# Attention ahead of the MLP products, in an order worked out by a list scheduler in the source

## The chip, the core and the metric

One core of one Trainium2 chip runs the whole program. The metric is device microseconds from the first to the last instruction of the kernel. TensorE (PE) does the matmuls, VectorE (DVE) and ScalarE (ACT) the element-wise work and the reads of PSUM, GpSimd (POOL) some element-wise work between SBUF tiles, SyncE (SP) issues the DMAs. Each engine runs its own instructions strictly in the order in which they stand in its queue, and waits on semaphores of the others.

## The reference

```
q, k, v: (2, 8, 768, 64) f32     scores = q k^T / 8, keys kept: the first n_sink = 4, and the window of 128
a = softmax(scores);  x = (a v), heads side by side: 1536 tokens x 512
h = x @ w_in (512 x 2048);  g = where(h > 0, h, exp(min(h, 0)) - 1);  x = g @ w_out (2048 x 512)
h = x @ w_in2;              g = max(h, 0) + alpha * min(h, 0);        out = g @ w_out2
```

The four weight matrices arrive as 64-bit floats.

## The kernel before, in words

**Attention.** A work item of attention is a *unit*: one or two blocks of 110 queries (`QB`) of one batch and one pair of heads. There are 32 units with 56 blocks, in the order batch, third of the sequence (`SPLIT`), pair of heads. For each unit PE computes the scores of both heads (tiles `qk`, line 521), DVE adds the mask and takes the row minimum of the negated scores (L529), ACT takes exponentials and their row sum (L534), DVE forms reciprocals (`st`, L544 and L547), POOL scales the rows (L551), PE transposes them against an identity (tiles `t`, L565), DVE or ACT copies the transposes to SBUF (tiles `pt`, L649), PE multiplies them by the values (tiles `x`, L586), and ACT and DVE split the result into a high and a low part (`xh` L594, `xl` L596), 512 rows by 1536 tokens.

**MLP.** Both layers run on split operands: each product is three matmuls (high with high, low with high, high with low; `matmul3`, L293). A *round* takes four of the 16 slices of 128 hidden features (`FG`): for a tile of tokens, four groups `h` of 12 matmuls (`g1`), the activation (`u`, L325 to L335; `gh` on ACT, `gl` on POOL), and four groups `o` of 12 (`g2`), which ACT (round 0) or DVE (L361) adds into `acc`. There are four rounds for each layer, eight in all. Rounds 1 to 7 use three tiles of 512 tokens (`TOK`); round 0 uses five narrower tiles (`TOK0`: 220, 220, 328, 440 and 328 tokens).

**Weights.** Each round needs eight *halves* of weights. A half is loaded as raw 64-bit numbers (L196) and decoded (`decode_w`): two operations on ACT (L267, L268), four on DVE (L270, L273, L276, L279), one on ACT (`wh`, L283), one on DVE (`wl`, L285).

**What sets the order.** While attention runs the order is written by hand (`manual_schedule`): a loop over steps `s` issues the scores of unit `s`, the values of unit `s - 2`, the transposes of unit `s - 1`, and at most one or two groups of round 0's first four tiles from the list `fill`; where there is none yet, `keep_busy` issues matmuls on the identity (L251). A decode that falls on a step issues its DVE operations together. Three softmax buffers (`SB`), five `pt` buffers (`PB`), and four PSUM banks each for `qk` and for everything else are in rotation. Then `mlp_rounds` issues round 0's last tile and rounds 1 to 7; with round 0's last tile it decodes all eight halves of round 1.

Of the kernel before, what the change touches and what calls it, by code (L numbers as in the profile page):

```python
# [11 lines left out]
F32 = mybir.dt.float32  # L12
# [33 lines left out]
NMAX0 = max(n for _, n, _ in TOK0)  # L46
# [17 lines left out]
FILL_MAX = 13  # L64
# [29 lines left out]
VCH = [sum(NCH[lo:hi]) for lo, hi in SPLIT]  # L94

# [18 lines left out]
def attention_mlp2(  # L114
# [38 lines left out]
    def load_kq(g, pool=None, queues=None):  # L153

        b, z, hp = sgs[g]
        nk, nq = KTOT[z], QTOT[z]
        if pool:
            t = pool.tile([P, 2 * max(KTOT)], F32, tag="kq", name=f"kq{g}", bufs=LB)  # L160
        else:
            t = room[:, g * 2 * nk : (g + 1) * 2 * nk]
        for e in range(2):
            rows = slice(e * D, e * D + D)
            lead = 2 * nk if e == 0 else 2 * nq
            c0 = KQ0[z] + e * nk
            src = kq[b, hp, rows, c0 : c0 + nk]
            src = bass.AP(src.tensor, src.offset, [list(src.ap[0]), [lead, 2], [1, nk]])
            (queues or (nc.sync, nc.sync))[e].dma_start(
                out=t[rows, : 2 * nk].rearrange("p (t c) -> p t c", t=2), in_=src  # L170
            )
        keys[g] = t

    def load_v(g, pool=None):
        b, z, hp = sgs[g]
        n = VCH[z] * 2 * D
        if pool:
            t = pool.tile([P, max(VCH) * 2 * D], F32, tag="vr", name=f"vr{g}", bufs=LB)
        else:
            t = room[:, HP * 2 * KTOT[0] + g * n :]  # L180
        nc.sync.dma_start(out=t[:, :n], in_=vc[b, hp, :, V0[z] : V0[z] + n])
# [18 lines left out]

    def load_w_early(g):
        o = HP * (2 * KTOT[0] + VCH[0] * 2 * D) + g * 2 * DM
        load_w(0, g, 0, room[:, o : o + 2 * DM].bitcast(I32).rearrange("p (n t) -> p n t", t=2))

    load_kq(0, queues=(nc.sync, nc.scalar))
    load_kq(1, queues=(nc.sync, nc.scalar))
    load_w_early(0)
    load_kq(2)
    load_w_early(1)
    load_v(0)  # L210
    load_kq(3)
    load_v(1)
# [40 lines left out]
    with tc.tile_pool(name="ps_warm", bufs=1, space=PSUM) as ps_warm:  # L253
        keep_busy(ps_warm, "busy", NWARM)
# [3 lines left out]
    def decode_w(wdec, pool, m, fc, io):  # L258
# [29 lines left out]
    def matmul3(out, pairs):  # L288
        n = 3 * len(pairs)
        i = 0  # L290
        for ah, al, bh, bl in pairs:
            for a, c in ((ah, bh), (ah, bl), (al, bh)):
                nc.tensor.matmul(out, a, c, start=(i == 0), stop=(i == n - 1))  # L293
                i += 1

    class Mlp:
# [3 lines left out]
        def __init__(self, gp, ps):  # L300
            self.gp, self.ps = gp, ps
            self.g, self.narrow = {}, 0

        def g1(self, m, c0, n, fc):
            t, big = c0, max(n, NMAX0)
            xh, xl = (x[:, :, c0 : c0 + n] for x in xs)
            wh, wl = wtiles[m, fc, 0]
            hp = self.ps.tile([P, 512], F32, tag="ps", name=f"h{m}_{t}_{fc}")[:, :n]
            matmul3(
# [7 lines left out]
            def after():  # L317
                u = tmp.tile([P, big], F32, tag="u", name=f"u{m}_{t}_{fc}")[:, :n]
                a, w, bufs = ("n", self.narrow, 2 * FG) if n <= self.narrow else ("", big, None)
                gh, gl = (  # L320
                    self.gp.tile([P, w], F32R, tag=f"g{c}{a}", name=f"g{c}{m}_{t}_{fc}", bufs=bufs)[:, :n]
                    for c in "hl"
                )
# [21 lines left out]
        def g2(self, m, c0, n, r, d):  # L345
            t = c0
            a = acc[:, d, c0 : c0 + n]
            po = self.ps.tile([P, 512], F32, tag="ps", name=f"o{m}_{t}_{r}_{d}")[:, :n]
# [6 lines left out]
            matmul3(po, pairs)  # L355
# [21 lines left out]
    def run(pieces):  # L377

        pend = []
        for p, extra in pieces:  # L380
            if p is None:
                done(pend.pop(0)())
                continue
            if extra:
                extra()
            pend.append(p())
# [10 lines left out]
    def mlp_rounds(mlp, items, wpools, wdec):  # L397
# [18 lines left out]
        for h in order[:2]:  # L416
            load_w(*h[1:])
        state = {"at": 0}

        def weights_step():  # L420
            j = state["at"]
            if j + 2 < len(order):
# [5 lines left out]
        for n, it in enumerate(items):  # L428
            mine = [lambda i=i, it=it: g1(*it, i) for i in range(FG)] + late
            late = [lambda d=d, it=it: g2(*it, d) for d in range(KC)]  # L430
            if n == 0:
                mine += [None] + late
                late = []
            step = len([p for p in mine if p]) // max(1, len(todo[it]))
            for j, p in enumerate(mine):
                if p is not None and todo[it] and j % step == 0:
# [5 lines left out]
        run(pieces)  # L442
# [7 lines left out]
    def distance(blk, pool=None):  # L450

        if pool:
            rel = pool.tile([P, 4 * QB], F32, tag="pt", name=f"rel{blk}", bufs=PB).bitcast(I32)
# [38 lines left out]
    def fast_path():  # L492
        outer = ExitStack()
        ps_qk = outer.enter_context(tc.tile_pool(name="ps_qk", bufs=4, space=PSUM))
        ps = outer.enter_context(tc.tile_pool(name="ps", bufs=4, space=PSUM))
        inner = ExitStack()
        ga = inner.enter_context(tc.tile_pool(name="ga", bufs=FG))
        at = inner.enter_context(tc.tile_pool(name="at", bufs=2))
        at2 = inner.enter_context(tc.tile_pool(name="wdec", bufs=2))
        mlp = Mlp(ga, ps)  # L500
        mlp.narrow = TOK0[0][1]
        soft, trans = {}, {}
        wraw.update(wfirst)
# [327 lines left out]
```

## Time and profile before

| what | value |
|---|---|
| median of 3 runs | 660.78 us (660.52 to 662.04) |
| span of the profiled execution | 660.5 us |
| PE, DVE, ACT, POOL busy | 96%, 66%, 48%, 31% of the span |
| bytes read from HBM | 49.01 MB |

The page gives no other time of the profiled execution than its span; the runs lie 0.0 to 1.5 us above it, their median 0.3 us. Busy time counts a pipelined matmul to its modelled end, so consecutive matmuls overlap in it; what a matmul really costs in a row of them is the distance from one start to the next.

### The profile page before, as it was taken

How to read it: one execution, taken by the hardware profiler on the slowest of the kernel's cores; microseconds unless marked ns; L12 is line 12 of the kernel's file. 1: busy time of each engine (PE TensorE's matmuls, PEld its weight loads, DVE VectorE, ACT ScalarE, POOL GpSimd, SP SyncE). 2: the span in 40 equal slices, each digit the busy share in tenths (PEclk: the TensorE clock that was granted, in tenths of full speed). 3: DMA queues.
4: the chain of work that ended last, by engine and by line, in shares of the span. 5: the costliest groups of instructions: out<-in, count | busy, mean ns of one | idle time of the engine just before them, and what ended most of it. 6: DMA issues, size and time to landing. Idle time of an engine off the chain costs nothing.

```text
span 660.5 us, 9670 instructions
## 1 busy us (share of the span) xinstructions
PE 633.7 (96%) x3444; PEld 526.6 (80%) x3444; DVE 435.9 (66%) x927; ACT 315.7 (48%) x719; POOL 204.4 (31%) x253
## 2 busy tenths in 40 slices
PE   8986899999989899999999999999999999999996
PEld 7775688887977677888888888888888888888885
DVE  5877767655399997768465876694669673343332
ACT  4877466655588675647545733453524230110010
POOL 3354334434123321233215453332123312331130
PEclk9988799999999999999999999999999999999999
DMA  8574336500043343121112211212222000000112
GB/s 256 149 213 140 106 85 167 158 25 1 34 159 127 124 132 128 37 91 64 65 58 70 65 64 44 84 65 65 64 65 64 33 0 1 2 0 1 64 50 83
DMA packets 21659, 52.87 MB, mean 80 GB/s; under 512 B 2658, under 2 KB 9826, under 8 KB 21602
## 3 DMA queue, kind: packets, MB, share of 16 engines
q1 hardware_dynamic: 21024, 51.93, 25.8%
q8 instruction: 29, 0.48, 0.3%
q10 hardware_dynamic: 578, 0.24, 0.2%
q14 instruction: 28, 0.23, 0.1%
HBM read 49.01 MB, written 3.15 MB: 79 GB/s over the span
## 4 chain that ended last, share of the span: by engine, by line
PE 78%; DVE 13%; ACT 4%; issue 2%; POOL 1%; DMA 1%; DVEq 0%; ACTq 0%; SPq 0%; POOLq 0%
PE o L293 36%; PE h L293 34%; PE x L586 3%; DVE wx L276 3%; DVE wx L279 2%; ACT s L534 2%; PE t L565 2%; PE qk L521 2%; DVE wl L285 2%; DVE wx L273 1%; DVE wx L270 1%; DVE pt L649 1%; DVE u L327 1%; DVE acc L361 1%; PE busy L251 1%
## 5 line engine op out<-in xcount | busy, mean ns | idle before, releaser
L340 POOL TENSOR_TENSOR gl<-u,gh 128x512 fp32r<-128x512 f32 (+3 forms) x104 | 133.1, 1280 | 327.6 <-ACT gh L339 322.5
L293 PE MATMUL o<-gh,wh 128*128 128x512 f32 (+3 forms) x416 | 157.3, 380 | 5.5 <-DVE u L327 5.5
L293 PE MATMUL h<-xh,wh 128*128 128x512 f32 (+3 forms) x416 | 158.1, 380 | 1.2 <-ACT xh L594 1.2
L293 PE MATMUL o<-gl,wh 128*128 128x512 f32 (+3 forms) x416 | 156.3, 376 | 1.8 <-POOL gl L340 1.7
L293 PE MATMUL h<-xl,wh 128*128 128x512 f32 (+3 forms) x416 | 156.6, 376 | 0.1
L293 PE MATMUL h<-xh,wl 128*128 128x512 f32 (+3 forms) x416 | 156.4, 376 | 0.0
L293 PE MATMUL o<-gh,wl 128*128 128x512 f32 (+3 forms) x416 | 155.8, 375 | 0.0
L339 ACT CAST gh<-u 128x512 fp32r<-128x512 f32 (+3 forms) x104 | 60.9, 585 | 139.3 <-DVE u L335 114.2
L293 PEld LDWEIGHTS o<-gh,wh 128*128 128x128 f32 x416 | 78.4, 189 | 23.4 <-DVE u L327 8.4
L361 DVE TENSOR_TENSOR acc<-o,acc 128x512 f32<-128x512 f32 x72 | 49.2, 688 | 72.0 <-PE o L293 71.7
L293 PEld LDWEIGHTS h<-xh,wh 128*128 128x128 f32 x416 | 79.2, 190 | 16.9 <-ACT xh L594 1.3
L293 PEld LDWEIGHTS o<-gl,wh 128*128 128x128 f32 x416 | 78.8, 189 | 16.0 <-POOL gl L340 2.9
L293 PEld LDWEIGHTS h<-xl,wh 128*128 128x128 f32 x416 | 79.3, 191 | 13.6 <-DVE xl L596 0.4
L293 PEld LDWEIGHTS h<-xh,wl 128*128 128x128 f32 x416 | 79.4, 191 | 13.4
L293 PEld LDWEIGHTS o<-gh,wl 128*128 128x128 f32 x416 | 78.8, 189 | 13.5
L551 POOL TENSOR_SCALAR s<-s,st 110x250 f32<-110x250 f32 (+5 forms) x112 | 52.6, 487 | 92.3 <-DVE st L547 31.1
L283 ACT CAST wh<-wx 128x512 fp32r<-128x512 f32 x64 | 39.6, 619 | 65.6 <-DVE wx L279 31.7
L534 ACT ACTIVATE s<-s,st 110x250 f32<-110x250 f32 (+5 forms) x112 | 53.1, 477 | 27.1 <-DVE st L529 27.0
L331 DVE TENSOR_SCALAR u<-h,alpha_sb 128x512 f32<-128x512 f32 x48 | 35.9, 748 | 45.6 <-PE h L293 45.6
L279 DVE CUSTOM_DVE_ANT_0 wx<-wx,wq 128x1024 uint16<-128x1024 uint16 x64 | 59.2, 925 | 1.4
L276 DVE SCALAR_TENSOR_TENSOR wx<-wr,wx 128x512 int32<-128x512 int32 x62 | 56.6, 914 | 1.0
L285 DVE TENSOR_TENSOR wl<-wx,wh 128x512 fp32r<-128x512 f32 x64 | 46.8, 733 | 15.5 <-ACT wh L283 13.9
(56 smaller groups left out, 634.5 us busy)
## 6 DMA issues: line engine op xcount, KB each, us to landing
wr<-in_w_dram SPq DMA_DIRECT2D x62, 512.0 KB, 3.6
kq<-in_kq_dram SPq DMA_DIRECT2D x16, 237.0 KB, 4.4
vr<-in_vc_dram SPq DMA_DIRECT2D x8, 384.0 KB, 4.1
out_dram<-acc SPq DMA_DIRECT2D x12, 256.0 KB, 2.0
kq<-in_kq_dram SPq DMA_DIRECT2D x16, 180.0 KB, 3.8
vr<-in_vc_dram SPq DMA_DIRECT2D x8, 256.0 KB, 3.8
acc<-in_w_dram SPq DMA_DIRECT2D x2, 512.0 KB, 5.4
kq<-in_kq_dram SPq DMA_DIRECT2D x8, 110.0 KB, 3.4
```

The source lines that it names most:

```text
L276: nc.vector.scalar_tensor_tensor(out=x, in0=high, scalar=-0x40000000, in1=x, op0=ALU.bitwise_and, op1=ALU.bitwise_or)
L279: nc.vector.tensor_tensor(out=x, in0=x, in1=r, op=ALU.add)
L283: nc.scalar.copy(wh, xf)
L285: nc.vector.tensor_tensor(out=wl, in0=xf, in1=wh, op=ALU.subtract)
L293: nc.tensor.matmul(out, a, c, start=(i == 0), stop=(i == n - 1))
L331: nc.vector.tensor_scalar(out=u, in0=hp, scalar1=0.0, scalar2=alpha_sb[:, fc : fc + 1], op0=ALU.min, op1=ALU.mult,)
L339: nc.scalar.copy(gh, u)
L340: nc.gpsimd.tensor_tensor(out=gl, in0=u, in1=gh, op=ALU.subtract)
L361: nc.vector.tensor_tensor(out=a, in0=po, in1=a, op=ALU.add)
L534: nc.scalar.activation(sb[:n, j, e, :w], sb[:n, j, e, :w], AF.Exp, bias=st[:n, 0, j, e : e + 1], scale=-1.0, accum_out=st[:n, 1, j, e : e ...
L551: nc.gpsimd.tensor_scalar(out=sb[:n, j, e, :w], in0=sb[:n, j, e, :w], scalar1=st[:n, 3, j, e : e + 1], scalar2=1.0, op0=ALU.mult, op1=ALU. ...
L586: nc.tensor.matmul(px[e * D : e * D + D, o : o + n], vr[:r, vs : vs + D], pt[:r, p0 : p0 + n], start=(k == 0), stop=(k == c - 1),)
```

## The change

The hand-written loop over steps is gone, and so are `TOK0` and `fill`. In its place each operation of attention, each weight half's decode (its eight operations one by one) and each load is given to `Plan` with a cost per engine, what it depends on and the buffers that it takes. `Plan.run` repeatedly picks the operation that can start earliest, by rank among those within 40 ns, issues it and books its end. Where PE would be idle for more than 0.7 us plus 128 ns it issues `keep_busy` matmuls. A copy `pt` may go to DVE or ACT. There are five softmax buffers and six `pt` buffers, eight PSUM banks shared by everything, and keys, values and early weights are placed anywhere in the space of `acc` (`Field`), which the MLP uses only later. Only two groups `h` of the first 512-token tile are part of the plan (`EARLY`), each in four parts. After it, `mlp_rounds` runs all eight rounds on 512-token tiles, and spreads the decodes for round 1 over round 0's three tiles. The program's scheduler may still move instructions of those rounds ahead on their engines, as the order below shows.

```diff
-TOK0 = [(0, 220, 0), (220, 220, 1), (440, 328, 2), (768, 440, 4), (1208, 328, 5)]
 TOK = [(c, 512) for c in range(0, NT, 512)]
-UB, SB, PB, LB = 2, 3, 5, 3
-MS = {2: 0, 3: 1, 4: 2}
-DS = [1, 3, 5, 7, 9, 10, 11, 12]
-NWARM, BUSYN = 10, 4
-FILL_MAX = 13
+UB, SB, PB = 2, 5, 6
+NBANK = 8
+BANKS = {"qk": 4, "tx": 4, "h": 2}
+NWARM = 10
+EARLY = 2
+WHEN = [16.0 + 3 * j for j in range(2 * FG)]
...
+class Plan:
+    SIGNAL, DRAIN, LAND, RATE, SLACK, GAP, IDLE = 60.0, 170.0, 1800.0, 230.0, 40.0, 700.0, 128.0
...
+    def best(self, todo):
+        cands = {}
+        for op in todo:
+            if any(d.end is None for d in op.deps) or op.behind and op.behind.end is None:
+                continue
+            asked = [cls.ask(size, len(holds)) for cls, size, *holds in op.takes]
+            if None in asked:
+                continue
+            for eng, cost in op.costs.items():
+                t = max([self.free.get(eng, self.start)] + [got[0] for got in asked])
+                for d in op.deps:
+                    t = max(t, d.end + (0.0 if d.eng == eng else self.SIGNAL))
+                if op.lock and eng in self.locks:
+                    t = max(t, self.locks["POOL" if eng == "DVE" else "DVE"])
+                cands.setdefault(eng, []).append((t, op, cost))
+        picks = []
+        for eng, got in cands.items():
+            first = min(t for t, _, _ in got)
+            t, op, cost = min((c for c in got if c[0] <= first + self.SLACK), key=lambda c: (c[1].rank, c[0]))
+            picks.append((t, op.rank, eng, op, cost))
+        return min(picks, key=lambda c: c[:3])
+    def run(self, idle):
+        todo = list(self.ops)
+        while todo:
+            t, _, eng, op, cost = self.best(todo)
+            if eng == "PE":
+                n = int((t - self.free.get("PE", self.start) - self.GAP) / self.IDLE)
+                if n > 0:
+                    idle(n, t)
...
+            op.fn(eng)
+            todo.remove(op)
+            op.eng = eng
+            op.end = self.free[eng] = t + cost
...
         nc.scalar.activation(xf, high.bitcast(F32), AF.Abs)
+        yield
         nc.scalar.activation(r, low.bitcast(U32), AF.Copy, scale=2.0**-29)
         yield
         nc.vector.tensor_scalar(out=xf, in0=xf, scalar1=EXP0, scalar2=None, op0=ALU.max)
+        yield
...
+            share = plan.add({"DVE": 230.0}, shares, deps=exps, rank=i - 3, lock=True)
...
+                    ns_.append(plan.add({"POOL": 250.0 + 0.8 * w}, normal, deps=[share], rank=i, lock=True))
...
+                copied.append(plan.add(
+                    {"DVE": 66.0 + 2.08 * c * nb, "ACT": 60.0 + 1.6 * c * nb}, copy, deps=[x],
+                    takes=[(pt_at, 1, hv[j])], frees=[ht], rank=i - 2,
+                ))
...
-        for s in range(nu + 2):
...
+        inner.enter_context(tc.manual_schedule())
+        plan.run(idle)
+        inner.close()
+        gb = outer.enter_context(tc.tile_pool(name="gb", bufs=2 * FG, reuse_waits="tile"))
+        mlp.gp = gb
+        mlp_rounds(mlp, [(k, t) for k in range(2 * NR) for t in TOK], (wa, wb), wdec, begun)
```

**On DVE, at a decode.** DVE's queue before, at a decode beside attention in the first batch's last third (the four DVE operations on `wx` are the decode, `pt` is the copy that a value product waits for):

```order
L596 TENSOR_TENSOR xl<-x_903,xh 128x220
L270 TENSOR_SCALAR wx_1_1_872<-wx_1_1_872 128x512
L273 TENSOR_SCALAR wx_1_1_872<-wx_1_1_872 128x512
L276 SCALAR_TENSOR_TENSOR wx_1_1_872<-wr_1_1_559,wx_1_1_872 128x512
L279 ISA wx_1_1_872<-wx_1_1_872,wq_1_1_873 128x1024
L649 COPY pt_6_940<-t_6_935 121x432
L544 TENSOR_SCALAR st_890<-st_890 110x4
L547 RECIPROCAL st_890<-st_890 110x4
```

The same kind of place in the change (a decode in the middle third; lines 407, 411 and 415 are the decode's, 827 is the copy, 867 `xl`, 771 the minima):

```order
L407 TENSOR_SCALAR wx_1_0_298<-wx_1_0_298 128x512
L411 SCALAR_TENSOR_TENSOR wx_1_0_298<-acc,wx_1_0_298 128x512
L867 TENSOR_TENSOR xl<-x_465,xh 128x220
L827 COPY pt_3_506<-t_3_488 122x440
L789 TENSOR_SCALAR st_428<-st_428 110x4
L792 RECIPROCAL st_428<-st_428 110x4
L415 ISA wx_1_0_298<-wx_1_0_298,wq_1_0_299 128x1024
L771 ISA s_495,st_496<-qk_0_497,mask 110x250
```

The decode's operations, which stood in one piece ahead of the copy, now stand apart, with the copy and the reciprocals between them. Of the 56 copies 28 stand on DVE and 28 on ACT, where 47 and 9 stood before.

**On PE, in the middle of attention.** PE's queue before, in the first batch's last third:

```order
L521 MATMUL qk_6_0_812<-kq_561 108x242
L521 MATMUL qk_6_1_814<-kq_561 108x242
L586 MATMUL x_820<-pt_2_781,vr_645 64x110 x4
L586 MATMUL x_820<-pt_3_788,vr_645 64x110 x4
L293 MATMUL h_220_0_835<-xh,wh_0_0_299 128x220
L293 MATMUL h_220_0_835<-xl,wh_0_0_299 128x220
L293 MATMUL h_220_0_835<-xh,wl_0_0_300 128x220
...
L565 MATMUL t_4_848<-ident,s_734 128x110 x4
```

In the change, in the same third (817 are transposes, 849 value products, 752 scores, 429 the MLP's matmuls):

```order
L817 MATMUL t_5_743<-ident,s_629 125x110 x4
L429 MATMUL h_0_0_754<-xh,wh_0_0_374 128x512
L429 MATMUL h_0_0_754<-xl,wh_0_0_374 128x512
L429 MATMUL h_0_0_754<-xh,wl_0_0_375 128x512
L817 MATMUL t_6_762<-ident,s_652 121x108 x4
L849 MATMUL x_771<-pt_4_739,acc 64x110 x4
L849 MATMUL x_771<-pt_5_759,acc 64x110 x4
L849 MATMUL x_786<-pt_6_780,acc 64x108 x4
L752 MATMUL qk_0_795<-acc 110x256
L752 MATMUL qk_1_796<-acc 110x256
```

A group of 12 narrow MLP matmuls stood after each unit; now only three wide ones stand here, and the next three follow after 13 other rows.

**On PE, at the end of attention.** In the change the last value product stands among the MLP's matmuls:

```order
L849 MATMUL x_1667<-pt_5_1664,acc 64x110 x4
L817 MATMUL t_6_1682<-ident,s_1568 121x108 x4
L429 MATMUL h_0_3_1785<-xh,wl_3_0_1435 128x512
L429 MATMUL h_0_3_1785<-xh,wh_3_0_1434 128x512
L429 MATMUL h_0_3_1785<-xl,wh_3_0_1434 128x512
...
L849 MATMUL x_1693<-pt_6_1690,acc 64x108 x4
L429 MATMUL h_0_3_1785<-xh,wl_3_0_1435 128x512
```

In PE's whole order 41 of the MLP's 2304 matmuls (2496 before, because of the narrow tiles) stand ahead of this last value product, and 55 more ahead of the first `o` group. Filler matmuls stand in three places (5, 1 and 1 of them) where 40 stood in the first five steps before.

## Rows read from the trace of the kernel before

**Rows 1.** The page, part 1 (busy, share) and part 2 (granted clock in tenths, 40 slices).
```profile
PE 633.7 (96%) x3444; PEld 526.6 (80%) x3444; DVE 435.9 (66%) x927; ACT 315.7 (48%) x719; POOL 204.4 (31%) x253
PEclk9988799999999999999999999999999999999999
```

**Rows 2.** Busy time by stretch, all engines; last three columns clock, DMA share, GB/s.
```profile
10.00:40.00 30.00, 28.75 (x275) 23.75 (x274) 24.63 (x101) 23.45 (x80) 14.17 (x30) 1.00 0.78 210
0.00:175.00 175.00, 160.12 (x1336) 135.19 (x1337) 112.84 (x439) 106.42 (x355) 68.79 (x153) 0.95 0.44 123
175.00:263.00 88.00, 81.57 (x382) 67.17 (x380) 83.71 (x133) 65.42 (x121) 22.13 (x16) 1.00 0.41 132
190.00:220.00 30.00, 28.94 (x129) 23.52 (x129) 29.62 (x46) 25.65 (x47) 8.85 (x6) 1.00 0.43 141
263.00:655.00 392.00, 391.86 (x1728) 324.25 (x1728) 238.69 (x355) 143.83 (x244) 113.46 (x84) 1.00 0.15 50
```

**Rows 3.** The chain that ended last, in time: start us, us, what.
```profile
6.26 0.73 PE qk L521 x4
...
99.71 0.75 PE qk L521 x8
...
121.39 1.04 PE qk L521 x8
122.43 0.96 PE x L586 x16
...
125.37 0.80 PE t L565 x8
...
263.14 11.18 PE o L293 x48
274.32 10.88 PE h L293 x48
...
633.37 21.77 PE o L293 x96
```

**Rows 4.** Busy in 0 to 175 us, instructions on tile u: DVE, ACT, POOL.
```profile
0.00:175.00 175.00, 7.23 (x16) 21.05 (x48) 13.53 (x16) 0.95 0.44 123
```

**Rows 5.** The same, the copies of line 649: DVE, ACT.
```profile
0.00:175.00 175.00, 26.00 (x47) 4.64 (x9) 0.95 0.44 123
```

**Rows 6.** The same, instructions on tile wx (decode): DVE, ACT.
```profile
0.00:175.00 175.00, 23.82 (x40) 10.19 (x16) 0.95 0.44 123
```

**Rows 7.** The same, line 359 (copies to acc): ACT.
```profile
0.00:175.00 175.00, 6.30 (x16) 0.95 0.44 123
```

**Rows 8.** Timeline of DVE: start us, us, instruction, in brackets the idle time before.
```profile
59.76 0.42 DVE L270 TENSOR_SCALAR wx<-wx 128x512 f32<-128x512 f32 x1
...
61.40 0.69 DVE L279 CUSTOM_DVE_ANT_0 wx<-wx,wq 128x1024 uint16<-128x1024 uint16 x1
62.01 0.60 DVE L649 COPY pt<-t 121x432 f32<-121x432 f32 x1
```

**Rows 9.** Timeline of PE, at a long wait and at a low clock.
```profile
62.67 0.99 PE L586 MATMUL x<-pt,vr 121*64 121x108 f32 x8 [3.51 <-DVE pt L649]
...
79.06 1.78 PE L565 MATMUL t<-ident,s 110*128 110x110 f32 x8
80.77 1.73 PE L521 MATMUL qk<-kq 64*110 64x256 f32 x8
82.43 1.03 PE L586 MATMUL x<-pt,vr 128*64 128x110 f32 x16
```

**Rows 10.** Busy by stretch, as rows 2, at the low clock.
```profile
78.00:80.00 2.00, 2.00 (x11) 2.00 (x11) 0.27 (x1) 0.47 (x2) 0.89 (x2) 0.50 0.50 153
```

**Rows 11.** Timelines of POOL and DVE, at a decode's last operation.
```profile
33.21 2.37 POOL L551 TENSOR_SCALAR s<-s,st 110x250 f32<-110x250 f32 x4 [4.00 <-PE x L586]
37.16 1.82 POOL L551 TENSOR_SCALAR s<-s,st 110x250 f32<-110x250 f32 x4 [0.97 <-PE qk L521]
...
33.20 0.68 DVE L285 TENSOR_TENSOR wl<-wx,wh 128x512 fp32r<-128x512 f32 x1
```

More of the change, by code (lines that the diff above doesn't have):

```diff
@@ new lines, with __init__, put, ask @@
+class Field:
+    def __init__(self, n):
+        self.n, self.held = n, []
+    def put(self, lo, size, uses):
+        hold = Hold(uses)
+        self.take(size, [hold], lo)
+        return hold
+    def ask(self, size, count=1):
+        best = None
+        for lo in [0] + [hi for _, hi, _ in self.held]:
+            over = [h for a, b, h in self.held if a < lo + size and b > lo]
+            if lo + size <= self.n and not any(h.left for h in over):
+                got = max([h.time for h in over], default=0.0), lo
+                best = min(best or got, got)
+        return best
+    def take(self, size, holds, lo):
+        self.held.append((lo, lo + size, holds[0]))
+        holds[0].slot = lo
@@ new lines, with __init__, ask, take @@
+class Cap:
+    def __init__(self, slots, most):
+        self.slots, self.most, self.holds = slots, most, []
+    def ask(self, size, count=1):
+        got = self.slots.ask(size, count)
+        room = self.most - count - sum(1 for h in self.holds if h.left)
+        if got is None or room < 0:
+            return None
+        ends = sorted((h.time for h in self.holds if not h.left), reverse=True)
+        return max(got[0], ends[room] if len(ends) > room else 0.0), got[1]
+    def take(self, size, holds, slots):
+        self.slots.take(size, holds, slots)
+        self.holds += holds
@@ L317, in after @@
             def after():
[L318 to L323, printed above, removed]
+                u = tmp.tile([P, n], F32, tag="u", name=f"u{m}_{t}_{fc}")
+                gh, gl = (self.gp.tile([P, n], F32R, tag=f"g{c}", name=f"g{c}{m}_{t}_{fc}") for c in "hl")
                 if m == 0:
@@ L421, in weights_step @@
             j = state["at"]
-            if j + 2 < len(order):
+            if j + 2 < len(order) and order[j + 2][1:] not in wraw:
                 load_w(*order[j + 2][1:])
@@ new lines, in fast_path, with high, low @@
+            va = plan.add(
+                {"PE": sum(2 * NCH[blk] for blk in blks) * 129.0}, values, deps=copied + [land_v[g]],
+                takes=[(kinds["tx"], 1, hx)], frees=hv + [hold_v[g]], rank=i - 3.0,
+            )
+            c0 = b * S + Q0[blks[0]]
+            def high(e_, tiles=tiles, o=o, hp=hp, c0=c0):
+                (nc.scalar.copy if e_ == "ACT" else nc.vector.tensor_copy)(
+                    xs[0][:, hp, c0 : c0 + o], tiles["x"][:, :o]
+                )
+            def low(e_, tiles=tiles, o=o, hp=hp, c0=c0):
+                nc.vector.tensor_tensor(
+                    out=xs[1][:, hp, c0 : c0 + o], in0=tiles["x"][:, :o], in1=xs[0][:, hp, c0 : c0 + o],
+                    op=ALU.subtract,
+                )
@@ new lines, in fast_path, with group @@
+            op = plan.add({"ACT": 60.0 + 0.75 * o}, high, deps=[va], frees=[hx], rank=i - 3)
+            rows[i] = plan.add({"DVE": 70.0 + 1.03 * o}, low, deps=[op], frees=[hx], rank=i - 3)
+        begun = []
+        for fc in range(EARLY):
+            hold, gen = Hold(1), []
+            def group(e_, fc=fc, hold=hold, gen=gen):
+                if not gen:
+                    gen.append(mlp.g1(0, *TOK[0], fc, hold.slot))
+                try:
+                    next(gen[0])
+                except StopIteration as end:
+                    begun.append(end.value)
+            op = None
+            for k in range(KC + 1):
+                deps = [split[fc]] + [
+                    rows[i] for i, (g, blks) in enumerate(units)
+                    if sgs[g][0] == 0 and sgs[g][2] == min(k, KC - 1) and Q0[blks[0]] < TOK[0][1]
+                ]
+                op = plan.add(
+                    {"PE": 680.0 if k < KC else 0.0}, group, deps=deps + ([op] if op else []),
+                    takes=[(kinds["h"], 1, hold)] if k == 0 else [], rank=100.0 + fc,
+                )
```

492 lines of the change are left out of this document (274 added, 218 removed).

## The prediction

> **What bounds the kernel now.** I read the page's busy shares first, then the stretches, then the chain that ended last. PE is busy 96% of the span [rows 1], but a busy PE says little here, so the stretches decide. Three stages show. From 263 us to the end PE is the bound and nothing else is: 391.86 of 392 us busy at full clock, while DVE has 239 us [rows 2], and the chain holds only PE, 10.88 us for 48 matmuls of 512 columns [rows 3], which is 0.2267 us each. From 175 to 263 us DVE is the bound: 83.71 of 88 us busy, and 29.62 of 30 us between 190 and 220 [rows 2]. There DVE decodes round 1's eight halves beside one 328-token tile and is late for the rest of that round. Up to 175 us attention and most of round 0 run together, and nobody is full: DVE 112.8, ACT 106.4, POOL 68.8 of 175 us [rows 2]. PE is nominally busy 160 us there, but part of that is filler and part ran at a lower clock (mean 0.95, and 0.50 in the low spells) [rows 2, 10]. A typical loss: the copy `pt` stands behind a decode on DVE, whose first operation starts at 59.76 and whose copy at 62.01 us [rows 8]; PE has meanwhile waited 3.51 us for that copy [rows 9].
>
> **The end is a sum of four terms.** Call T the time at which PE reaches the last value product in the changed order. Behind it stand 2304 - 41 = 2263 matmuls of 512 columns. So time = T + 2263 x 0.2267 + stalls in the first MLP rounds + tail. The second term is 513.0 us, at the price of [rows 3], which holds for both layers there. The tail is what lies behind the last matmul: the last 96 begin at 633.37 and take 21.77 us [rows 3], so 655.1 of 660.5, 5.4 us; the change leaves these last additions and stores as they are.
>
> **T, from what each engine must do by then.**
> - PE: a unit of two wide blocks costs 1.04 for scores, 0.96 for values, 0.80 for transposes, 2.80 us [rows 3]. For each pair of heads and batch there are two such units, one unit with one block (taken as half, 1.40) and one of a narrow and a wide block (0.75 for scores [rows 3], and 12 instead of 16 parts of the rest, 1.32: 2.07). That is 9.07 us, eight times: 72.6. With 41 wide MLP matmuls, 9.3, PE has 81.9 us.
> - DVE: the 112.8 us up to 175 us [rows 2] held all of attention and eight decodes. The activations go out (7.2) [rows 4]; 19 copies move to ACT (19 x 26.00/47 = 10.5) [rows 5]; five of 40 decode operations stand behind T (3.0) [rows 6]; two wide `u` come in (0.45 each by [rows 4], at 512 instead of some 302 columns 0.77: 1.5). 93.6 us.
> - ACT: 106.4 [rows 2] less 21.1 [rows 4] and 6.3 [rows 7], plus 19 copies at 4.64/9 = 0.52 (9.8) [rows 5], less two `wh` (1.3) [rows 6], plus four wide operations on `u` (0.74 each, scaled as above: 3.0): 90.6 us.
> - POOL: 68.8 - 13.5 = 55.3 us [rows 2, 4].
> - DMA: 123 GB/s over 175 us is 21.5 MB [rows 2]. Three of the weight loads fewer, but the same order of bytes, in 115 us is at most 187 GB/s; 210 were moved between 10 and 40 us [rows 2]. I cost it at nothing; what hides it is the loads' lead over their unit. If that goes, each late load stops PE for part of a unit, 1 to 2 us.
>
> PE's first scores start at 6.26 us [rows 3], and all of this can hardly start earlier. The fullest engine is DVE. T is 6.3 + 93.6 divided by the share of that time in which DVE works. The trace shows two shares. Where it waited on the attention chain, in 10 to 40 us, it was 24.63/30 = 0.82 [rows 2], which gives T = 120; where it had a backlog, 0.987 [rows 2], T = 101. No row shows the new order. I take 0.86, near the lower one, because three engines are now nearly even (82, 91 and 94 us) and each hands work to the others, but above it, because the new order removes what cost most in that stretch: decode operations no longer stand as one piece of 2.25 us (59.76 to 62.01) ahead of a copy [rows 8], and five softmax buffers instead of three let scores run ahead. T = 6.3 + 93.6/0.86 = 115.
>
> **The other edits.** The narrow tiles go: their extra matmuls cost nothing in the sum, since all 2304 are counted at the wide price. Decoding one operation at a time adds no operation. Fillers fall from 40 to 7 matmuls, and 33 identity matmuls less on PE is not a gain by itself; their cover was the clock, see below. The first rounds: after T, 55 wide matmuls stand on PE ahead of the first `o`, 12.5 us. By then DVE must do 17 operations (0.60 each by [rows 6]: 10.2), ACT one `gh` and POOL one `gl` (0.85 by [rows 4], about 1.4 at 512 columns), some 12.3 with ACT's 0.7, and the group needs them only behind its ninth matmul, 2 us later. So nothing to 5 us is lost here; I take 1.5. The eight decodes of round 1 now lie beside 65 us of matmuls (288 x 0.2267), 24 us of DVE [rows 6], so the DVE-bound stretch should vanish. If it came back as before (88 us for 79.4 us of matmuls: 96 of 328 tokens, 14.1, and 288 wide ones) [rows 2], it would cost 8.6 us, not 1.5.
>
> Sum: 115.0 + 513.0 + 1.5 + 5.4 = **634.9 us** against a span of 660.5. The runs' median lies 0.3 above that span, so 635.2.
>
> **POOL and DVE against each other.** When a decode's last operation ran at 33.20 for 0.68 us, POOL's four scalings took 2.37 us instead of 1.82: 0.55 us for one meeting [rows 11]. The planner keeps such pairs apart by its own clock; on the chip they may meet. A price for all of them follows from the counts: 35 decode operations, 64 on `st` and 10 on masks are 109; each finds on average half of one POOL scaling ahead of it, 1.82/4/2 = 0.23 us [rows 11], so at most 25 us more on DVE.
> [...]
>
> **The rivals.**
> [...]
> - *The low clock*, the one that ends slower. With the fillers and the narrow groups gone PE has short waits everywhere in attention. The clock fell to 0.50 before after waits such as the 3.51 us one [rows 9, 10]. At 0.50, transposes and scores of a unit take 1.71 + 1.66 (79.06 to 82.43) instead of 0.80 + 1.04 [rows 3, 9], 1.83 times. If all of attention ran so, PE would need 81.9 x 1.83 = 150 us, T = 156 and the time 676. It decides from T = 140.6 on; with some 18 us of waits on top, that is when about half of PE's work runs low. Against it: the order has a filler in only three places, so the plan sees no PE wait of over 0.83 us elsewhere.
> - *The decode backlog comes back* (or the new order only shifts the stall behind T): 8.6 instead of 1.5, 642.
> - *DVE near full*: T = 101, no stall: 619.
>
> **How the numbers follow.** A measurement of this kernel tells about 0.3% (2 us) from no change. The forecast (T 106 to 124, stalls up to 5) has 0.66 and gives 626 to 645; DVE near full 0.08; the backlog 0.08; half-way meetings or a clock that falls several times (643 to 656) 0.10; no change 0.02; slower by the clock 0.06. Faster therefore 0.92, within 0.3% 0.02, slower 0.06. The range from 620 to 654 leaves out the last two cases and the ends of the others.
>
> **What would show it.** Right: DVE about 0.86 busy up to the last value product, that product near 115 us, PE at 48 per 10.88 us behind it with gaps of a few us, no filler to speak of. Wrong: spells of granted clock 0.5 in attention; minima, `st` or decode operations on DVE lengthened beside POOL; PE waits on `pt` of over 2 us; a gap at the first `o` group; DVE above 95% after attention.

## The result, and the profile after

The changed kernel takes 628.6 us (median of 4 runs, 628.26 to 629.2) against 660.78 us before; the ratio is 0.952, 95% interval 0.950 to 0.954. The profiled execution spans 626.7 us. A run's time lies 1.7 to 2.0 us above the span of the same execution wherever both are known (628.51 and 626.7 here), so the span of 660.5 before belongs to an execution of some 662.3 us, one of the longest: the fall is 33.8 us in spans and 32.2 us in medians. The page of the changed kernel, parts 1 and 2 (40 slices of the span, busy share in tenths) and the shares of the chain that ended last:

```profile
span 626.7 us, 9131 instructions
PE 615.6 (98%) x3186; PEld 498.4 (80%) x3186; DVE 427.0 (68%) x900; ACT 316.5 (51%) x706; POOL 204.3 (33%) x245
...
DVE  5988998999567938494658868764968483344331
...
PEclk9999999999999999999999999999999999999999
...
PE 91%; ACT 5%; DVE 2%; POOL 1%; issue 1%; POOLq 0%; ACTq 0%
```

The low spells of the third to fifth slice [rows 1] are gone. The next view is busy time by stretch, as in [rows 2]: start and end, length, then PE, weight loads, DVE, ACT and POOL with their instructions, granted clock, DMA share, GB/s.

```profile
20.00:40.00 20.00, 18.68 (x166) 12.25 (x166) 17.18 (x74) 16.02 (x58) 10.72 (x23) 1.00 0.71 178
40.00:60.00 20.00, 19.94 (x208) 14.87 (x210) 17.43 (x87) 16.36 (x68) 10.44 (x24) 1.00 0.80 209
60.00:100.00 40.00, 39.36 (x377) 28.61 (x373) 38.58 (x158) 38.75 (x132) 22.71 (x47) 1.00 0.66 191
...
110.00:150.00 40.00, 39.21 (x174) 32.14 (x173) 39.26 (x58) 33.09 (x61) 13.30 (x10) 1.00 0.38 132
150.00:200.00 50.00, 50.00 (x222) 41.44 (x221) 34.87 (x56) 33.60 (x61) 13.37 (x10) 1.00 0.29 96
300.00:621.00 321.00, 321.00 (x1417) 265.86 (x1417) 193.41 (x286) 103.11 (x174) 91.32 (x68) 1.00 0.14 47
6.30:106.53 100.23, 96.81 (x895) 68.89 (x895) 90.13 (x390) 87.20 (x309) 52.98 (x112) 1.00 0.71 194
```

In attention DVE and ACT are now at 0.96 and 0.97 of the time from 60 to 100 us. The last row runs up to T, the start of the last value product: DVE works 90.13 of 100.23 us, 0.90, where it had 0.64 over the first 175 us before [rows 2]. From 110 to 150 us DVE is full (0.98) and PE loses almost nothing. PE's waits of the whole execution (us in total, times, longest), and its timeline at T and at the longest wait behind T:

```profile
PE x L849 <- ACT pt L827: 1.6, 5, 0.5
PE busy L383 <- POOL ident masks.py:199: 1.5, 1, 1.5
PE t L817 <- POOL s L804: 0.8, 2, 0.5
PE o L429 <- POOL gl L472: 0.8, 1, 0.8
PE qk L752 <- DMA acc<-in_kq_dram: 0.2, 1, 0.2
```

```profile
106.53 0.60 PE L849 MATMUL x<-pt,acc 121*64 121x108 f32 x8
...
121.70 0.39 PE L429 MATMUL o<-gh,wh 128*128 128x512 f32 x1
122.88 0.50 PE L429 MATMUL o<-gl,wh 128*128 128x512 f32 x1 [0.79 <-POOL gl L472]
```

No wait for `pt` is over 0.5 us, where one took 3.51 [rows 9]. The one wait behind attention stands at the first `o` group. From there the chain holds only PE, as from 263.14 before [rows 3]:

```profile
121.03 1.81 POOL gl L472
...
122.88 8.91 PE o L429 x38
131.79 10.88 PE h L429 x48
```

**The forecast's sum, kernel by kernel.** T is read from PE's timeline, n is the number of `h` matmuls that start ahead of T, the share is DVE's busy time between 6.3 and T, the sum is T + (2304 - n) x 0.2267 + 5.4. All kernels have wide tiles throughout; the runs are told below.

| kernel | T | n | T - 0.2267 n | DVE's share | sum | span |
|---|---|---|---|---|---|---|
| changed kernel | 106.53 | 41 | 97.2 | 0.899 | 625.0 | 626.7 |
| e1, three softmax buffers | 109.48 | 38 | 100.9 | 0.855 | 628.6 | 629.3 |
| e2, decode in one piece | 107.68 | 45 | 97.5 | 0.920 | 625.2 | 625.9 |
| e3, planner's lock off | 113.99 | 43 | 104.2 | 0.868 | 632.0 | 632.6 |
| e4, round 1 decoded late | 106.91 | 41 | 97.6 | 0.894 | 625.3 | 626.1 |
| e5, no group in the plan | 107.30 | 9 | 105.3 | 0.913 | 633.0 | 633.7 |
| e6, four groups | 107.25 | 48 | 96.4 | 0.911 | 624.1 | 624.8 |
| e7, no fillers | 110.65 | 42 | 101.1 | 0.867 | 628.8 | 630.9 |
| f1, e4 and e6 | 107.13 | 48 | 96.2 | 0.913 | 624.0 | 624.6 |
| f2, f1 and a truer price | 108.26 | 57 | 95.3 | 0.878 | 623.1 | 623.7 |
| f3, copies on DVE | 119.65 | 57 | 106.7 | 0.901 | 634.4 | 637.3 |

Eight of the eleven spans lie 0.6 to 0.8 above their sum. The changed kernel, e7 and f3 lie 1.7 to 2.9 above, and these three are the ones in which PE waits at the first `o` group (0.8, 1.0 and 1.6 us). Of the 0.6 to 0.8, 0.5 is the last value product itself, which the sum leaves out (it starts at 106.53, the next matmul at 107.06). So only one quantity is left to explain: T less the MLP work that PE does by then.

### The profile page after: what moved, and what is told of

It reads as the page before. It is cut to its first block, busy times and chain, and to the rows that moved or that the text cites. A ratio compares the mean times of both kernels' runs of the same rounds, so it can differ in the third digit from the quotient of the medians.

```text
span 626.7 us, 9131 instructions
## 1 busy us (share of the span) xinstructions
PE 615.6 (98%) x3186; PEld 498.4 (80%) x3186; DVE 427.0 (68%) x900; ACT 316.5 (51%) x706; POOL 204.3 (33%) x245
## 4 chain that ended last, share of the span: by engine, by line
PE 91%; ACT 5%; DVE 2%; POOL 1%; issue 1%; POOLq 0%; ACTq 0%
PE o L429 41%; PE h L429 39%; PE t L817 3%; PE qk L752 3%; PE x L849 3%; ACT s L779 3%; PE busy L383 1%; POOL s L804 1%; ACT pt L827 1%; DVE wx L415 0%; DVE wx L411 0%; ACT wx L399 0%; DVE wl L421 0%; POOL gl L472 0%; ACT wh L419 0%
## 5 line engine op out<-in xcount | busy, mean ns | idle before, releaser
L472 POOL TENSOR_TENSOR gl<-u,gh 128x512 fp32r<-128x512 f32 x96 | 132.3, 1379 | 339.5 <-ACT gh L471 331.8
L429 PE MATMUL o<-gl,wh 128*128 128x512 f32 x384 | 149.5, 389 | 0.8 <-POOL gl L472 0.8
L429 PE MATMUL h<-xh,wh 128*128 128x512 f32 x384 | 150.1, 391 | 0.0
L429 PE MATMUL h<-xh,wl 128*128 128x512 f32 x384 | 149.6, 390 | 0.0
L429 PE MATMUL h<-xl,wh 128*128 128x512 f32 x384 | 149.5, 389 | 0.0
L429 PE MATMUL o<-gh,wh 128*128 128x512 f32 x384 | 149.4, 389 | 0.0
L429 PE MATMUL o<-gh,wl 128*128 128x512 f32 x384 | 149.4, 389 | 0.0
L471 ACT CAST gh<-u 128x512 fp32r<-128x512 f32 x96 | 59.4, 620 | 131.6 <-DVE u L467 114.2
L429 PEld LDWEIGHTS h<-xh,wl 128*128 128x128 f32 x384 | 72.1, 188 | 15.0
L804 POOL TENSOR_SCALAR s<-s,st 110x250 f32<-110x250 f32 (+5 forms) x112 | 53.0, 493 | 46.8 <-DVE st L792 18.4
L463 DVE TENSOR_SCALAR u<-h,alpha_sb 128x512 f32<-128x512 f32 x48 | 35.9, 747 | 45.6 <-PE h L429 45.6
L421 DVE TENSOR_TENSOR wl<-wx,wh 128x512 fp32r<-128x512 f32 x64 | 48.4, 758 | 20.2 <-ACT wh L419 18.4
L401 ACT ACTIVATE wq<-wr 128x512 int32<-128x512 uint32 x62 | 41.6, 672 | 33.3 <-DVE wx L415 28.6
L415 DVE CUSTOM_DVE_ANT_0 wx<-wx,wq 128x1024 uint16<-128x1024 uint16 x64 | 55.9, 873 | 1.2
```

The costliest lines, as they stand in the source:

```text
L421: nc.vector.tensor_tensor(out=wl, in0=xf, in1=wh, op=ALU.subtract)
L463: nc.vector.tensor_scalar(out=u, in0=hp, scalar1=0.0, scalar2=alpha_sb[:, fc : fc + 1], op0=ALU.min, op1=ALU.mult,)
L471: nc.scalar.copy(gh, u)
L472: nc.gpsimd.tensor_tensor(out=gl, in0=u, in1=gh, op=ALU.subtract)
L804: nc.gpsimd.tensor_scalar(out=s[:n, j, e, :w], in0=s[:n, j, e, :w], scalar1=st[:n, 3, j, e : e + 1], scalar2=1.0, op0=ALU.mult, op1=ALU.mult,)
```

## The experiments

All ratios are against the kernel before, which ran beside each set at 660.45 to 660.65 us.

**e1. Three softmax buffers.**

```diff
-UB, SB, PB = 2, 5, 6
+UB, SB, PB = 2, 3, 6
```

> The changed kernel with three softmax buffers instead of five; the planner plans with three. Theory (DVE and ACT were nearly full in the second half of attention, because five buffers let minima and exponentials run ahead and because the short operations are woven one by one): with three buffers both wait more on the chain; T, the start of the last value product, goes from 106.5 towards the 115 that a DVE share of 0.86 gives; the time from 628.6 to 631 to 637. Rival (the buffers hardly matter, the planner's weaving fills the engines with three as well): T within 2 us of 106.5 and the time 627 to 630.

Measured: 630.91 us (630.81 to 631.27), ratio 0.955 (0.954 to 0.957). T is 109.5 and DVE's share falls to 0.855, in busy time up to T:

```profile
6.30:109.48 103.18, 98.80 (x902) 70.10 (x903) 88.24 (x388) 87.17 (x309) 51.25 (x112) 1.00 0.71 188
```

The theory holds at the lower edge of its range: two more buffers are worth 3 us of T and 2.3 us of the time. The order with three softmax buffers is still 30 us faster than before, so these two buffers are a small part.

**e2. A decode's four DVE operations in one piece.**

```diff
-                next(gen[0], None)
+                for _ in range(n):
+                    next(gen[0], None)
...
-                ("ACT", 560.0), ("ACT", 570.0), ("DVE", 336.0), ("DVE", 336.0), ("DVE", 609.0), ("DVE", 602.0),
-                ("ACT", 525.0), ("DVE", 601.0),
+                ("ACT", 560.0), ("ACT", 570.0), ("DVE", 1883.0), ("ACT", 525.0), ("DVE", 601.0),
```

> The changed kernel with the four DVE operations of a weight decode as one operation of the plan (1.88 us), as in the kernel before; everything else is planned. Theory (a decode in one piece in front of a copy or a minimum makes PE wait and costs DVE's chain): PE waits on pt of over 1 us come back, T rises by 3 to 8 us, and the time is 631 to 637. Rival (the planner puts the piece where nothing urgent stands behind it, and DVE has the same work): T within 2 us of 106.5, the time 627 to 630.

Measured: 628.89 us (627.63 to 629.2), ratio 0.952 (0.950 to 0.953), no change. PE's waits on `pt` did not come back:

```profile
PE x L849 <- ACT pt L827: 0.7, 2, 0.5
PE x L849 <- DVE pt L827: 0.6, 2, 0.5
```

My theory falls. A piece of 1.9 us on DVE does no harm where the planner chooses its place and may give the next copy to ACT; which of these two freedoms does it is not shown.

**e8. The kernel before, with the decode behind the copies.** The same suspicion, tried alone in the hand-written order: in a step with a decode, its DVE operations follow the copies and the reciprocals.

```diff
-            if s in decodes:
-                next(decodes[s])
             take = 1 if fill and fill[0][0] <= s else 0
...
                 normalised(s)
+            if s in decodes:
+                next(decodes[s])
```

> The kernel before with one thing altered: in a step with a decode, its four DVE operations stand behind the copies and the reciprocals instead of ahead of them. Theory (the decode ahead of the copy was a typical loss: PE waited 10.8 us on pt in all, and ran at a granted clock of 0.50 behind the long ones): most of these waits and the low spells go, and the time falls by 5 to 12 us to 649 to 656. Rival (the decode is only late elsewhere: the weights of round 0 or the next minima come later by 2.25 us a time, or the other ends of the hand-written order bind): within 2 us of 660.8, or slower.

Measured: 670.38 us (669.71 to 670.64), ratio 1.014 (1.013 to 1.016), 1.4% slower. PE's waits, and its timeline at the longest of them:

```profile
PE x L586 <- DVE pt L647: 4.7, 6, 1.3
PE qk L521 <- DVE st L529: 3.6, 3, 2.0
PE h L293 <- ACT wh L283: 2.0, 1, 2.0
```

```profile
78.64 1.48 PE L521 MATMUL qk<-kq 64*108 64x242 f32 x4 [1.99 <-DVE st L529]
80.93 0.99 PE L586 MATMUL x<-pt,vr 121*64 121x108 f32 x8 [0.81 <-DVE pt L647]
...
87.53 2.03 PE L521 MATMUL qk<-kq 64*110 64x256 f32 x8
89.49 1.79 PE L586 MATMUL x<-pt,vr 128*64 128x110 f32 x16
```

The waits on `pt` fell from 10.8 to 4.7 us, as wanted. But the minima now stand behind the decode, the scores wait for them and the weights come late. Behind these waits the granted clock was 0.50 from 80 to 90 us, and scores and value products took 2.03 and 1.79 us in this view, where the chain has 1.04 and 0.96 [rows 3] at a clock of 1.00. The last value product came at 172.4 instead of 164.0 us. The rival holds: a fixed order only moved the loss.

**e3. A planner that lets DVE and POOL overlap.**

```diff
-                if op.lock and eng in self.locks:
+                if False:
                     t = max(t, self.locks["POOL" if eng == "DVE" else "DVE"])
```

> The changed kernel with a planner that does not keep DVE's and POOL's operations on SBUF apart. [...] Theory (meetings happen anyway, since the chip drifts from the planner's clock, and cost little; the lock itself holds operations back): the time within 3 us of 628.6, either way, and the means of DVE's operations within 5%.

Measured: 635.3 us (632.63 to 637.05), ratio 0.962 (0.959 to 0.964). The time lies 6.7 us above the changed kernel's, outside the theory's 3 us, as it would if meetings cost DVE a part of the prediction's 25 us. The trace says otherwise. A decode's last operation on `wx` (minimum, median and maximum in ns), and busy time up to T and in one stretch of it:

```profile
L415 DVE CUSTOM_DVE_ANT_0 wx<-wx,wq x6: 660/694/851, 20.1 to 105.1; 128x1024 uint16<-128x1024 uint16 x6
```

```profile
6.30:113.99 107.69, 102.41 (x894) 71.91 (x894) 93.50 (x396) 89.09 (x310) 56.24 (x112) 0.95 0.67 185
...
14.00:16.00 2.00, 2.00 (x15) 1.45 (x12) 0.77 (x2) 1.47 (x3) 1.54 (x4) 0.50 0.97 236
```

The same operation had a median of 660 ns in the changed kernel. Up to T the minima and the two operations on `st` have the same means in both runs (L771 383, L789 189, L792 175 ns), so for 64 of the prediction's 109 operations nothing changed. Longer are the decode's operations (L415 749 instead of 669 ns, L421 753 instead of 709) and POOL's scalings (L804 521 instead of 493). As far as a meeting lengthens an operation, as in [rows 11], meetings up to T cannot have cost more than 3.4 us on DVE (93.50 against 90.13, with six instructions more) and 3.3 on POOL, far from the 25 of the prediction.

Behind T the changed kernel itself has such meetings, with POOL's longer `gl`. POOL's timeline, and the chain in the same stretch:

```profile
108.04 3.00 POOL L472 TENSOR_TENSOR gl<-u,gh 128x512 fp32r<-128x512 f32 x2 [3.92 <-ACT gh L471]
117.27 1.38 POOL L472 TENSOR_TENSOR gl<-u,gh 128x512 fp32r<-128x512 f32 x1 [6.24 <-ACT gh L471]
```

```profile
109.81 1.79 DVE wx L411
...
113.71 0.61 DVE wx L411
...
114.35 0.69 DVE wx L415
...
117.55 1.68 DVE wx L415
```

Each kind of decode operation stands there once at its usual length and once 1.0 to 1.2 us longer, ending 0.6 us behind a `gl`. The two long ones lie on the chain that ends in PE's wait at the first `o` group, so by the chain meetings had a part in those 0.8 us; no run took them away there.

What stands out up to T in e3 is the clock: 0.95 instead of 1.00. Over the five runs the span follows the mean clock:

| mean clock | 0.993 | 0.991 | 0.989 | 0.985 | 0.984 |
|---|---|---|---|---|---|
| span, us | 630.8 | 632.6 | 633.5 | 634.0 | 635.2 |

A line through them gives some 629 us at 0.998, the clock of the changed kernel (626.7); this is an estimate from five points. By it some 4 of the 6.7 us go with the clock, and 2 to 3 are left for the meetings and the other order. Whether the meetings in turn lower the clock I did not separate. One difference stands where the clock first falls (0.76 from 12 to 14 us, 0.50 from 14 to 16): this plan put 2 fillers there (from 9.59 us on; each is two matmuls in the trace), the changed kernel's put 6, and with none, in e7 below, the clock falls near the same place (0.79 from 10 to 12 us).

**e7. No fillers in PE's waits.**

```diff
         def idle(n, t):
+            return
```

> The changed kernel without the seven identity matmuls that the plan puts into PE's waits (the ten at the start stay). Theory (the clock stays at 1.00 because PE's waits in the new order are short, 0.5 us at most, not because of seven fillers): clock 1.00 throughout and the time within 1 us of 628.6. Rival (the clock falls where the fillers stood): a stretch at granted clock 0.50, T later by 1 to 5 us, the time 629.5 to 634.

Measured: 631.52 us (629.86 to 632.64), ratio 0.955 (0.953 to 0.957). PE's timeline at the place, and the stretch behind it:

```profile
8.89 0.81 PE L752 MATMUL qk<-acc 64*110 64x110 f32 x6 [0.21 <-DMA acc<-in_kq_dram]
10.90 1.80 PE L817 MATMUL t<-ident,s 110*110 110x110 f32 x6 [1.19 <-POOL s L804]
```

```profile
12.00:24.00 12.00, 11.74 (x71) 7.80 (x70) 7.79 (x31) 7.88 (x25) 4.97 (x13) 0.50 0.69 186
```

The changed kernel at the same place:

```profile
9.26 1.38 PE L383 MATMUL busy<-ident 128*128 128x128 f32 x10
```

The rival holds. Where the changed kernel has fillers PE now waits 1.19 us, the granted clock falls (0.79 from 10 to 12 us, 0.50 from 12 to 24, 0.80 from 24 to 26; 1.00 from 12 to 24 in the changed kernel), and T comes 4.1 us later in this execution, the longest of the five. Across runs the clock was 0.988 to 0.997 and the span 630.9 to 628.0.

**e4. Round 1 decoded with round 0's last tile.**

```diff
-                todo[of_round[j * len(of_round) // len(hs)]].append((wpools[(k + 1) % 2], *h))
+                todo[of_round[-1 if k == 0 else j * len(of_round) // len(hs)]].append((wpools[(k + 1) % 2], *h))
```

> The changed kernel with all eight halves of round 1 decoded with round 0's last 512-token tile, as in the kernel before, instead of spread over its three tiles. Theory (the backlog of DVE in that stretch was a cost of its own, some 8 us of the gain: PE not working 9 us before, 0.8 after): 24 us of decodes on DVE fall beside 22 us of matmuls, round 1 waits on weights or on its activations, and the time is 634 to 640, with T unchanged at 106.5. Rival (the program's scheduler and the wide tiles remove the backlog wherever the decodes stand): 627 to 630.

Measured: 627.35 us (626.98 to 627.84), ratio 0.950 (0.948 to 0.951). The theory falls: with wide tiles the eight decodes may even stand together, and the wait at the first `o` group is gone, since fewer decode operations stand ahead of its activations: DVE ends the second `u` behind T at 116.6 instead of 120.1 us. Spreading the decodes was no part of the gain.

**e5 and e6. No group, and four groups, of MLP matmuls in the plan.**

```diff
-EARLY = 2
+EARLY = 0
```

and for e6

```diff
-BANKS = {"qk": 4, "tx": 4, "h": 2}
+BANKS = {"qk": 4, "tx": 4, "h": 4}
...
-EARLY = 2
+EARLY = 4
```

> The changed kernel with no group of MLP matmuls inside the plan (24 matmuls of 512 columns, 5.4 us of PE, go behind it). Theory (T is set by DVE and ACT, PE has slack in attention): T falls by at most 1.5 us (two activations of u less on ACT and DVE), PE does the 5.4 us behind it, and the time is 631 to 634. Rival (PE is what attention waits for): T falls by 5 us and the time stays at 627 to 630.

> The changed kernel with four groups of MLP matmuls inside the plan instead of two, and four PSUM banks for them. Theory (PE has slack in attention, DVE and ACT set T): 5.4 us of PE's work more is done in waits, two more activations cost DVE and ACT 1.5 us; T rises by 1 to 3 us, and the time falls to 624 to 628. Rival (PE is what attention waits for): T rises by 5.4 us and the time stays at 627 to 631.

Measured: e5 637.88 us (635.51 to 639.62), ratio 0.966 (0.963 to 0.968); e6 626.65 us (626.4 to 627.94), ratio 0.949 (0.947 to 0.950). T stays within 0.8 us in both (107.30 and 107.25), though PE has 7.3 us less (n = 9) or 1.6 us more (n = 48) to do by then: PE does not set T, as the theory said; in e5 the plan put 21 fillers into PE's waits up to T instead of 7. The size for e5 was too small: the program's scheduler, too, put fewer `h` matmuls ahead of T, and the runs in which the clock fell added up to 4 us (spans 633.7 at clock 1.000, 637.7 at 0.992). For e6 only 7 matmuls more came ahead of T, not 24: the scheduler had already filled most of the room.

**f3. All copies on DVE.**

```diff
-                    {"DVE": 66.0 + 2.08 * c * nb, "ACT": 60.0 + 1.6 * c * nb}, copy, deps=[x],
+                    {"DVE": 66.0 + 2.08 * c * nb}, copy, deps=[x],
```

> The changed kernel with all 56 copies pt on DVE; 28 of them leave ACT. Theory (DVE sets T together with ACT, and the sharing of copies was worth it): DVE has 28 x 0.53 = 14.8 us more, 90.1 + 14.8 = 104.9 us by T; at a share of 0.90 as in the changed kernel T is 123 and the time 645, at 0.987 T is 112.6 and the time 635; so 634 to 646. Rival (PE's own chain or POOL's scalings set T, DVE had room): T at most 110, the time 627 to 632.

Measured: 639.2 us (638.05 to 639.29), ratio 0.967 (0.966 to 0.969). Busy time up to T:

```profile
6.30:119.65 113.35, 109.36 (x953) 78.54 (x953) 102.15 (x418) 79.18 (x283) 51.51 (x112) 0.98 0.60 171
```

DVE has 12.0 us more to do by T and T comes 13.1 us later, with the same share as in the changed kernel, 0.901 against 0.899. ACT, relieved to 79.18 us, gives nothing back. So DVE sets T, at least where its work grows; no run took work from DVE alone. Sharing the copies is one of the parts that carry the gain, though less than this run's 10.6 us: it takes back 28 copies, and the change had moved 19.

**f4. Narrow tiles in round 0.**

```diff
+TOK0 = [TOK[0]] + [(c, 256) for c in range(512, NT, 256)]
...
-        mlp_rounds(mlp, [(k, t) for k in range(2 * NR) for t in TOK], (wa, wb), wdec, begun)
+        mlp_rounds(mlp, [(k, t) for k in range(2 * NR) for t in (TOK if k else TOK0)], (wa, wb), wdec, begun)
```

> The changed kernel with the second and third tile of round 0 cut into four of 256 tokens. By the rows of the kernel before, a matmul takes 0.2267 us with 512 columns, 0.153 with 328 and 0.111 with 220 from start to start: about 0.014 us each that does not shrink with the columns, so about 0.121 with 256. Theory (narrow tiles cost PE this and nothing else here): 384 x 0.121 - 192 x 0.2267 = 2.9 us, T as before, the time 630.5 to 632.5. Rival 1 (their activations and additions, each with a fixed part, bring DVE's backlog back): over 633. Rival 2 (what they cost lies in waits that are there anyway): within 1 us of 628.6.

Measured: 634.4 us (633.91 to 634.7), ratio 0.960 (0.959 to 0.961). PE's timeline at the first `o` group and in a row of 256-column matmuls:

```profile
116.89 0.49 PE L430 MATMUL o<-gh,wh 128*128 128x512 f32 x1 [0.83 <-ACT gh L472]
118.35 0.50 PE L430 MATMUL o<-gl,wh 128*128 128x512 f32 x1 [0.97 <-POOL gl L473]
...
120.10 0.63 PE L430 MATMUL o<-gh,wh 128*128 128x512 f32 x1
120.53 0.63 PE L430 MATMUL o<-gl,wh 128*128 128x512 f32 x1
...
141.02 0.28 PE L430 MATMUL h<-xl,wh 128*128 128x256 f32 x1
141.14 0.28 PE L430 MATMUL h<-xh,wl 128*128 128x256 f32 x1
```

A 256-column matmul takes 0.120 us from start to start, as expected: 2.6 us for all 384. T is 106.12. The rest is rival 1 in a small form: the four narrow `h` groups ahead of the first `o` give less cover (48 x 0.107 = 5.1 us), PE waits twice there, and behind the waits the granted clock falls (mean 0.95 from 110 to 120 us, 0.88 from 120 to 130) and seven matmuls from 119.25 us on take 0.43 instead of 0.23 us.

**f1 and f2. The better parts together.** f1 has the edits of e4 and e6; f2 besides books the two reciprocal operations at what the trace shows.

```diff
-            share = plan.add({"DVE": 230.0}, shares, deps=exps, rank=i - 3, lock=True)
+            share = plan.add({"DVE": 370.0}, shares, deps=exps, rank=i - 3, lock=True)
```

> Four MLP groups inside the plan and, besides, all halves of round 1 decoded with round 0's last tile: the two edits that were each a little faster than the changed kernel (626.65 and 627.35 against 628.6). Theory (the one saves PE work behind T, the other removes the 0.8 us wait and the gap of the first o group, which are different places): T about 107, 48 groupwise matmuls ahead of it, and the time 624 to 626.4. Rival (both removed the same wait at the first o group): 626.4 to 627.5, as with four groups alone.

> The kernel of the run before, with one price of the planner set to what the trace shows: the pair of reciprocal operations on DVE costs 0.37 us from start to start (42.27 to 42.64), the planner books 0.23. Theory (the order is bound by what engines can do, and a truer clock of the planner lets fewer operations come late): T falls by 0.5 to 3 us, the time 621 to 626. Rival (the order is one of many about as good, and T scatters by 1 to 3 us either way with any price): as likely above as below 625.

Measured: f1 626.72 us (626.5 to 627.07), ratio 0.949 (0.947 to 0.950), no better than e6: the rival holds, both edits removed the wait at the first `o` group. f2 took 625.87 us (625.65 to 626.29), ratio 0.947 (0.946 to 0.949), the fastest of all, 0.4% under the changed kernel. But T did not fall, it rose to 108.3; nine more matmuls came ahead of it (57 against 48, 2.0 us). So the gain is real and the reason that I gave for it is not shown.

## Why the prediction was right, point by point

- **The sum of four terms** held, and not only for the kernel that it was made for. 2263 matmuls behind T was exact (n = 41). The tail is 5.3 us (the last 96 matmuls end at 621.4). The step from span to run time was wrong: not 0.3 but 1.8 us, so that the working, 634.9 of span, stood for some 636.7.
- **T, the mis-sized term**: 106.5 instead of 115. "I take 0.86" was the step that was off. DVE's share was 0.899, which is 93.6/0.86 - 93.6/0.899 = 4.7 us; and its work between 6.3 us and T was 90.1 instead of 93.6, another 3.9 us: some 1.7 of the 112.8 us had been done ahead of 6.3 us, and the rest of the difference I did not trace. Together 8.6, against 8.5 measured.
- **That DVE sets T** was right as far as it was tried: f3 moved T with DVE's work at the same share, e5 and e6 left it where it was with PE's work changed.
- **The two reasons for a share above 0.82** fared differently. Five buffers instead of three: right, 3 us of T, and with three the share is 0.855, just the 0.86 of the forecast. The decode no longer in one piece: wrong, e2 shows no effect, and e8, which only moves the piece, a loss. I took one visible wait [rows 8, 9] for the cause. That the planner's free choice of place and engine stands in its place is argued; only the choice of engine has a run (f3).
- **The first rounds**: 1.5 us forecast; the span lies 1.75 above the sum, 0.5 of it the last value product. DVE is still full from 110 to 150 us (0.98), one of the prediction's signs of being wrong, as is the wait at the first `o` group; but PE has work of its own there and loses little, and by e4 it would not lose more with the decodes in their old round. f4 points to wide tiles against narrow ones instead; narrow tiles together with late decodes were not run in the new order.
- **Fillers**: "33 identity matmuls less on PE is not a gain by itself; their cover was the clock" was right as far as e7 tried it: without the few that are left the clock was 0.50 from 12 to 24 us and the time 2.9 us longer.
- **The narrow tiles at nothing**: right for the sum, since it counts wide matmuls only; what 256-token tiles cost is 5.8 us in f4, 2.6 of it PE's own.
- **The rivals**: DVE full over all of attention did not come, but nearly so from 60 to 100 us (0.96). No run shows the price of up to 25 us for meetings or the half-way meetings of the chances; what e3 shows is at most 3.4 us on DVE up to T, as far as meetings lengthen operations. The low clock did not come in the changed kernel, but e7 loses by it, and e3 at least in part; both stay far below the 676 us of that rival.
- **DMA at nothing**: right, PE waited 0.2 us for keys, at 194 GB/s up to T, where at most 187 had been forecast.

Where the 33.8 us of span came from can be read by stretch. Before, T was 164.04, with 336 narrow MLP matmuls ahead of it:

```profile
164.04 0.60 PE L586 MATMUL x<-pt,vr 121*64 121x108 f32 x8 [0.70 <-DVE pt L649]
```

From start to start a matmul took 0.113 us with 220 columns, 0.149 with 328 and 0.201 with 440 (medians on PE's timeline), so these are 45.6 us, and T less the MLP work was 118.4 against 97.2 now: 21.2 us. The 480 narrow matmuls cost 4.3 us more than the 288 wide ones in their place. What the span lies above the sum falls from 10.1 to 1.8, which makes the other 8.3 us, near the 8.6 that the prediction's working gives for the stretch from 175 to 263 us [rows 2]. These are estimates from the two traces.

How the 21.2 us divide between planning the order, sharing the copies and the clock is not settled. Counted as time that PE lost, the clock has at most some 9 of them (0.05 x 175 us, by the mean clock of 0.95 [rows 2], an estimate). Each part taken away in e1, e3, e5, e7, f3 and f4 cost 2 to 11 us, and the parts lean on each other. No run took back the eight shared PSUM banks, the sixth `pt` buffer or the new places of keys, values and weights, and none gave them to the hand-written order; so the planned order is not shown apart from them.

## What to carry to other kernels

Write the time as a short sum of terms that each have a row, and put the doubt into one number; here that number was the busy share of the engine with the most work, and it moves with the buffers (0.855 with three softmax buffers, 0.899 with five), so it is better taken from a stretch that has the new kernel's. A wait that is visible in the trace is not yet a cause: move the work that it waits for before believing it. In an order where nothing has slack, look at the granted clock of every variant first, since a short wait can cost several microseconds behind it (in e7 a wait of 1.19 us, and T 4.1 us later).

## What the runs showed of the hardware

- One 1.19 us wait of PE near the start was followed by some 13 us at a granted clock of 0.50 (e7), and two waits of 0.83 and 0.97 us by seven matmuls of 0.43 instead of 0.23 us and a mean clock of 0.88 from 120 to 130 us (f4); the 0.79 us wait of the changed kernel was followed by none (1.00 from 122 to 128 us). The same program differed from execution to execution: in e5 the mean clock was 0.992 to 1.000 and the span 637.7 to 633.7 us, some 0.5 us for each 0.001.
- Up to T, PE counts as busy 96.81 of 100.23 us and yet does not set T: 32 matmuls of 0.2267 us fewer left it where it was (e5). Part of what counts as busy lies beside weight loads that wait: those of the transposes waited 10.4 us for POOL's scalings up to T, and a row of eight transposes took 0.96 to 1.75 us; in the row of 1.75 three such waits of 0.15 to 0.25 us stand. The waits of the weight loads up to T, and two such rows:

```profile
PEld t L817 <- POOL s L804: 10.4, 36, 0.7
```

```profile
30.64 1.75 PE L817 MATMUL t<-ident,s 110*125 110x110 f32 x8
...
64.40 0.96 PE L817 MATMUL t<-ident,s 110*110 110x110 f32 x8
```

- VectorE's operations were longer beside GpSimd's: beside a `gl` of 1.4 to 1.5 us a decode operation of 0.61 or 0.69 us took 1.79 or 1.68 (the changed kernel behind T). Up to T, beside scalings of some 0.5 us, letting them meet added at most 3.4 us to DVE's busy time (e3).
